# The second MLP matmul as seven half-size products (2x2 Strassen form) in a fused attention and MLP kernel

## The chip, the cores and the metric

The kernel runs on one core of a Trainium2 chip. The metric is the device time of one execution in microseconds (us), of which each kernel has several runs. A profile of one execution goes with it; its span (first to last instruction) is some 2 us shorter than the time (1.7 to 2.9 us in the runs of this study). Engines are named as the profile names them: PE is TensorE, PEld its weight loads, DVE is VectorE, ACT is ScalarE, POOL is GpSimd, SP is the engine that mostly issues DMAs.

## The reference

Eight batches of 576 rows go through an attention with separate softmaxes for q and k, then through a layer norm and a two-layer MLP with a residual. Cut to what matters:

```python
q_s = softmax(q, axis=-1)                 # q, k, v: (8, 8, 576, 64) fp32
k_s = softmax(k, axis=2)
x   = q_s @ (k_s^T @ v)                   # per batch and head, then (8, 576, 512)
xn  = (x - mean(x)) / sqrt(var(x) + 1e-6) * g_ln
out = x + maximum(xn @ w_ch1, 0.0) @ w_ch2   # w_ch1: 512 x 2048, w_ch2: 2048 x 512
```

## The kernel before

The rows are cut into nine chunks of 512. Chunks 0 to 7 hold the first 512 rows of each batch. Chunk 8 (`C9`) gathers the 64 rows that each batch has left over. For each chunk the first MLP matmul makes `ph = w1^T xn^T`, a ReLU writes it to `hT` (hidden index on the partitions, 16 slices of 128), and the second matmul takes slices of `hT` as weights against `w2_sb`. The attention work of the next chunk is issued in between as "side" work, at given places of the stream of matmuls.

```python
def cast_v(b, j, eng=None):               # fp32 v to bf16, for the k^T v product
    ...
    if eng is nc.scalar:
        nc.scalar.copy(dst, raws[b][1][:, hs])
    else:
        nc.vector.tensor_copy(out=dst, in_=raws[b][1][:, hs])

def stats(c, t, src):                     # layer norm of row tile t
    nc.vector.bn_stats(st[:, t], src)
    nc.vector.bn_aggr(mv[:, t], st[:, t])
    nc.vector.scalar_tensor_tensor(xn[:, t], in0=src, scalar=mv[:, t, 0:1], in1=g_bc, ...)

def y_out(c, t, pc, cols=slice(0, 512), eng=None):
    ...
    nc.vector.scalar_tensor_tensor(ot, in0=pc, scalar=rstds[c][:, t:t+1], in1=xs[c][0][:, t, cols], ...)
    eng = eng or nc.gpsimd
    if c < B:
        eng.dma_start(out[c, 0:SM, :].rearrange("(p t) n -> p t n", t=T)[:, t, cols], ot)
    else:                                  # chunk 8: 2 x 64 rows, one store for each batch
        for half in range(2):
            eng.dma_start(out[2*t + half, SM:S, cols], ot[64*half : 64*half + 64])

def mm2(c, t, ko):                         # 4 row tiles x 16 slices, 512 wide
    ...
    nc.tensor.matmul(hbox["pc"], hbox["h"][:, ko, t, :], w2_sb[:, ko, :],
                     start=(ko == 0), stop=(ko == KO2 - 1))
    if ko == KO2 - 1:
        y_out(c, t, hbox["pc"])

# main loop, chunk 1 (cut)
side += prep_side(2, 16, 46)               # exp of q and k, cast_v of batch 2
side += attn_side(2, 46, 62, 63, 87)       # attention of batch 2
side += [(40, lambda: load_batch(3))]
...
```

The last row tile of chunk 8 is done in two halves of 256 columns (`mm2_last`), so that little is left to store at the very end. POOL issues most stores.

The softmax here doesn't subtract the row's maximum and nothing guards it: scores larger than these inputs give would overflow.

## Time and profile before

| what | value | read from |
|---|---|---|
| time, median of 3 runs | 301.36 us (299.45 to 301.83) | times |
| span of the profiled run, granted clock | 297.7 us, 1.000 | page |
| PE busy | 284.4 us, 96% | page, part 1 |
| chunks 1 to 6 | 29.75 to 29.80 us each | start of each chunk's first matmul |
| chunk 7, chunk 8 | 29.38, 27.83 us | same |
| after the last matmul ("tail") | 4.24 us | same |

Parts 1 and 2 of the page of the kernel before. Each digit of a row of part 2 is a fortieth of the span, in tenths busy.

```profile
PE 284.4 (96%) x1679; PEld 147.3 (49%) x1697; DVE 179.7 (60%) x392; ACT 131.7 (44%) x242; POOL 30.8 (10%) x63
PE   6869988999999999999999999999999999999994
DVE  4556588437995975397539753975399258820021
PEclk9999999999999999999999999999999999999999
```

PE is the bound, at full clock, from chunk 1 (the eighth slice) on.

The next view cuts the same run into stretches, here chunk 1, chunk 3, chunk 8 and the tail. Its first line names the columns; a count of instructions stands in brackets.

```profile
core 0: us, PE busy (x) PEld busy (x) DVE busy (x) ACT busy (x) POOL busy (x), PEclk, DMA share, GB/s
57.53:87.28 29.75, 29.57 (x163) 14.48 (x164) 21.53 (x51) 17.49 (x34) 2.25 (x5) 1.00 0.79 221
...
117.08:146.87 29.79, 29.69 (x163) 14.47 (x164) 19.66 (x44) 13.64 (x25) 2.24 (x4) 1.00 0.92 221
...
265.63:293.46 27.83, 27.78 (x144) 13.98 (x143) 4.87 (x7) 8.36 (x14) 3.71 (x7) 1.00 0.16 38
293.46:297.70 4.24, 0.00 (x0) 0.00 (x0) 0.48 (x1) 0.00 (x0) 0.00 (x0) 0.98 0.28 63
```

PE has 0.1 to 0.2 us of idle time in a chunk of 29.8 us. DVE has 20 to 22 us of work in chunks 1 to 3.

Last, the tile query for `vm`, the bf16 copy of v, in chunks 1 and 2 (duration in ns as minimum, median, maximum):

```profile
L149 DVE CAST vm<-vt x12: 410/420/477, 64.0 to 108.4; 128x512 bf16<-128x512 f32 x12
```

### The profile page before, as it was taken

To read this page: it belongs to the slowest core of one execution; us is meant where nothing else is said; L and a number is where in the kernel's file an instruction comes from. 1 tells how busy PE (TensorE), PEld (TensorE's weight loads), DVE (VectorE), ACT (ScalarE), POOL (GpSimd) and SP (SyncE) were. 2 spreads that over 40 slices of the span, in tenths; PEclk is the share of its full clock that TensorE was granted. 3 is DMA by queue.
4 is the path that set the end of the run, shared out by engine and by line. 5 is a ranking of instruction groups with operands and counts; after the bars stand their busy time and mean duration, and the time that the engine had idled before them with its cause. 6 is when DMAs were issued, how large, how long until landed. Compare 5 with 4: busy or idle time off the path is not lost.

```text
span 297.7 us, 4354 instructions
## 1 busy us (share of the span) xinstructions
PE 284.4 (96%) x1679; PEld 147.3 (49%) x1697; DVE 179.7 (60%) x392; ACT 131.7 (44%) x242; POOL 30.8 (10%) x63
## 2 busy tenths in 40 slices
PE   6869988999999999999999999999999999999994
PEld 2658654445445444544454445444544444444443
DVE  4556588437995975397539753975399258820021
ACT  3538783396254560475047504750471054015300
POOL 3500020200010011001100110011000100110021
PEclk9999999999999999999999999999999999999999
DMA  7999999948968993999599629962017201120033
GB/s 195 216 208 271 289 157 237 318 139 242 296 138 222 333 138 128 306 262 184 130 309 223 124 90 311 221 141 73 35 35 124 90 35 37 53 88 35 2 70 70
DMA packets 73942, 48.97 MB, mean 164 GB/s; under 512 B 42241, under 2 KB 71681, under 8 KB 73922
## 3 DMA queue, kind: packets, MB, share of 16 engines
q1 hardware_dynamic: 66050, 34.74, 48.6%
q0 software_dynamic: 7872, 13.96, 18.9%
q8 instruction: 13, 0.21, 0.3%
q14 instruction: 7, 0.06, 0.1%
HBM read 36.70 MB, written 9.44 MB: 155 GB/s over the span
## 4 chain that ended last, share of the span: by engine, by line
PE 86%; DMA 5%; ACT 3%; DVE 3%; issue 1%; SPq 1%; POOL 0%; ACTq 0%
PE ph L344 37%; PE pc L393 36%; PE pc L404 3%; DMA qt<-in_q_dram 3%; PE pkv L241 2%; PE ph L359 2%; PE po L273 2%; DMA kt_98<-in_k_dram 2%; PE pc L415 1%; PE ptr L511 1%; DVE xn L299 1%; ACT ek L139 1%; DVE st L297 1%; PE po L280 1%; ACT hT L332 1%
## 5 line engine op out<-in xcount | busy, mean ns | idle before, releaser
L344 PE MATMUL ph<-xnT,w_sb 128*128 128x512 bf16 x528 | 128.1, 379 | 0.0
L332 ACT ACTIVATE hT<-ph 128x512 bf16<-128x512 f32 x115 | 68.4, 597 | 106.2 <-PE ph L344 106.1
L393 PE MATMUL pc<-w_sb,hT 128*128 128x512 bf16 x481 | 109.4, 379 | 0.7
L393 PEld LDWEIGHTS <-hT 128*128 128x128 bf16 x496 | 47.8, 98 | 58.3 <-DVE hT L330 2.3
L344 PEld LDWEIGHTS <-w_sb 128*128 128x128 bf16 x528 | 48.0, 98 | 50.5 <-DMA xnT<-xn 0.3
L375 DVE SCALAR_TENSOR_TENSOR ot<-pc,rstd,x 128x512 f32<-128x512 f32 (+1 forms) x37 | 27.1, 733 | 39.6 <-PE pc L393 31.2
L381 POOL DMA_DIRECT2D out_dram<-ot x32 | 18.1, 564 | 203.4 <-DVE ot L375 191.4
L273 PE MATMUL po<-kv_sb,eqT 128*128 128x128 bf16 x128 | 24.3, 219 | 1.5 <-DVE kv_sb L250 0.8
L189 DVE TENSOR_REDUCE zq<-eq 128x8 f32<-128x512 bf16 x34 | 22.4, 660 | 3.6 <-ACT eq L180 3.6
L330 DVE TENSOR_SCALAR hT<-ph 128x512 bf16<-128x512 f32 x17 | 11.7, 685 | 21.2 <-PE ph L344 21.1
L299 DVE SCALAR_TENSOR_TENSOR xn<-x,mv,g_bc 128x512 bf16<-128x512 bf16 x30 | 22.5, 752 | 1.1
L241 PE MATMUL pkv<-vm,ek 128*128 128x129 bf16 x112 | 22.6, 220 | 0.4 <-DVE vm L149 0.3
L297 DVE BATCH_NORM_STATS2 st<-x 128x6 f32<-128x512 bf16 x30 | 20.8, 694 | 1.0
L273 PEld LDWEIGHTS <-eqT 128*128 128x128 bf16 x128 | 11.7, 98 | 13.2 <-issue 1.9
L172 ACT ACTIVATE eq<-qt 128x512 bf16<-128x512 f32 x24 | 13.3, 619 | 10.4 <-DMA qt<-in_q_dram 10.4
L311 DVE TENSOR_TENSOR x<-po,rq 128x512 bf16<-128x512 f32 x26 | 17.8, 683 | 0.2
L404 PE MATMUL pc<-w_sb,hT 128*128 128x512 bf16 x61 | 15.6, 379 | 0.2
L139 ACT ACTIVATE ek<-kt 128x512 bf16<-128x512 f32 x28 | 15.5, 619 | 0.1
L247 DVE RECIPROCAL rzk<-pkv 128x2 f32<-128x2 f32 x14 | 2.4, 171 | 20.1 <-PE pkv L241 20.1
L149 DVE CAST vm<-vt 128x512 bf16<-128x512 f32 x26 | 10.2, 421 | 5.7 <-DMA vt<-in_v_dram 5.5
L468 PE MATMUL warm<-junk 128*128 128x256 bf16 (+1 forms) x59 | 11.0, 329 | 1.2 <-DVE junk L560 1.2
L241 PEld LDWEIGHTS <-ek 128*128 128x128 bf16 x112 | 10.6, 98 | 1.9 <-issue 0.8
(79 smaller groups left out, 178.3 us busy)
## 6 DMA issues: line engine op xcount, KB each, us to landing
out_dram<-ot POOLq DMA_DIRECT2D x32, 256.0 KB, 3.8
qt<-in_q_dram SPq DMA_DIRECT2D x7, 1024.0 KB, 12.5
vt<-in_v_dram SPq DMA_DIRECT2D x7, 1024.0 KB, 9.7
kt<-in_k_dram SPq DMA_DIRECT2D x6, 1024.0 KB, 7.5
w_sb<-in_moe_w_ch_dram POOLq DMA_DIRECT2D x8, 512.0 KB, 9.8
kt_98<-in_k_dram SPq DMA_DIRECT2D x4, 288.0 KB, 5.6
qt<-in_q_dram SPq DMA_DIRECT2D x2, 512.0 KB, 6.5
kt<-in_k_dram SPq DMA_DIRECT2D x2, 512.0 KB, 8.3
```

The lines of the kernel that those rows point to most:

```text
L139: nc.scalar.activation(eks[b][:, :, hs, :].rearrange("p t h d -> p h t d"), kt[:, hs], AF.Exp)
L189: nc.vector.reduce_sum(zq[:, t], eq[:, t], axis=AX.X)
L241: nc.tensor.matmul(pkv[:, j % 2, 0:w], lhsT, rhs, start=(t == 0), stop=(t == last))
L273: nc.tensor.matmul(pobox["p"][:, i * P : i * P + P], eqTs[c][:, t, i, :], kv_sb[:, c, i, :], start=True, stop=True,)
L297: nc.vector.bn_stats(st[:, t], src)
L299: nc.vector.scalar_tensor_tensor(xn[:, t], in0=src, scalar=mv[:, t, 0:1], in1=g_bc, op0=ALU.subtract, op1=ALU.mult,)
L332: nc.scalar.activation(dst, src, AF.Relu)
L344: nc.tensor.matmul(hbox["ph"], w1_sb[:, ko, m * P : (m + 1) * P], xnTs[c][:, :, ko, :], start=(ko == 0), stop=(ko == KO1 - 1),)
L375: nc.vector.scalar_tensor_tensor(ot, in0=pc, scalar=rstds[c][:, t : t + 1], in1=xs[c][0][:, t, cols], op0=ALU.mult, op1=ALU.add,)
L381: eng.dma_start(out[c, 0:SM, :].rearrange("(p t) n -> p t n", t=T)[:, t, cols], ot)
L393: nc.tensor.matmul(hbox["pc"], hbox["h"][:, ko, t, :], w2_sb[:, ko, :], start=(ko == 0), stop=(ko == KO2 - 1),)
L404: nc.tensor.matmul(hbox["pc", t], hbox["h"][:, ko, t, :], w2_sb[:, ko, :], start=(ko == 0), stop=(ko == KO2 - 1),)
```

## The change

For chunks 2 to 8 the second matmul is written as a 2x2 block product. Its blocks are the two halves of the rows, the even and odd slices of the contraction, and the two halves of the columns. The Strassen-Winograd form needs seven block products in place of eight. Each is 2 row tiles x 8 slices of matmuls 256 columns wide, so 64 matmuls of 512 columns become 112 of 256: seven eighths of the columns. The price is four sums of blocks of `hT` per chunk (on DVE, eight instructions), partial sums that ACT copies into other PSUM banks or SBUF and DVE adds, and, once for the whole kernel, four differences of blocks of `w2_sb` (on POOL, sixteen instructions). To find the memory, the buffers of k and v are single. The order of the side work is new, and so is the store of chunk 8. From chunk 2 on ACT also does the ReLUs that DVE had, and from batch 4 on the casts of v. The diff, cut to its core:

```diff
+    w2_q = const.tile([P, 4, KH, DH2], BF16)
...
+            raw.tile([P, H, T, D], FP32, tag="kt", name="kt", bufs=1),
+            raw.tile([P, H, T, D], FP32, tag="vt", name="vt", bufs=1),
...
+    def quarter_w2(i, g):                       # 16 times, in chunk 1
+        ...
+        dst, x, y = ((t1, b12, b11), (t3, b22, b12), (t2, b22, t1), (t4, b21, t2))[i]
+        nc.gpsimd.tensor_sub(out=dst, in0=x, in1=y)
...
+    def sum_h(g, i):                            # 8 times per chunk
+        dst, x, y, op = (
+            (s1, a21, a22, ALU.add), (s2, s1, a11, ALU.subtract),
+            (s3, a11, a21, ALU.subtract), (s4, a12, s2, ALU.subtract),
+        )[i]
+        nc.vector.tensor_tensor(out=dst, in0=x, in1=y, op=op)
...
+    def store_rest(eng, t, cols):               # chunk 8
+        eng.dma_start(out[2 * t : 2 * t + 2, SM:S, cols], ybox[C9, t][:, cols])
...
+        product(1, "a", first=True, at={
+            0: [lambda i=i: sum_h(1, i) for i in range(4)], 15: [seed_c]})
+        product(5, "b", first=True)
+        product(6, "a", at={15: [lambda: copy_u("s2")]})
+        product(2, "c", last=True, at={7: [seed_e]})
+        product(7, "a", at={2: ys("c", 0, 0)[:1], 5: ys("c", 0, 0)[1:], 15: [lambda: copy_u("s3")]})
+        product(3, "e", last=True, at={13: [lambda: add_u("b", "s3")]})
+        product(4, "a", last=True, at={
+            1: ys("e", 1, 0)[:1], 4: ys("e", 1, 0)[1:],
+            7: ys("b", 1, 2)[:1], 10: ys("b", 1, 2)[1:], 15: ys("a", 0, 2)})
...
             if c == 1:
                 side += prep_side(2, 16, 46)
                 side += attn_side(2, 46, 62, 63, 87)
+                side += [(40, lambda: load_batch(3, (2,))), (50, lambda: load_batch(3, (0, 1)))]
+                side += prep_side(3, 96, 127, sums=False)
+                side += [
+                    (4 + 7 * (4 * i + g), lambda i=i, g=g: quarter_w2(i, g))
+                    for i in range(4) for g in range(4)
+                ]
```

More of the change, by code (lines that the diff above doesn't have):

```diff
@@ L49 @@
     NP = H // 2
+    KH = KO2 // 2
+    DH2 = DM // 2
     VW = P + 2
     C9 = B
+    FAST = 2
     T0 = 6
@@ L73 @@
     ones_f = const.tile([1, P], FP32)
-    g_row = const.tile([1, DM], FP32)
-    v0 = const.tile([P, H, T0, D], BF16)
     g_bc = const.tile([P, DM], FP32)
@@ L101, in alloc_batch @@
         raws[b] = (
-            raw.tile([P, H, T, D], FP32, tag="kt", name="kt"),
-            raw.tile([P, H, T, D], FP32, tag="vt", name="vt"),
+            raw.tile([P, H, T, D], FP32, tag="kt", name="kt", bufs=1),
+            raw.tile([P, H, T, D], FP32, tag="vt", name="vt", bufs=1),
             raw.tile([P, H, T, D], FP32, tag="qt", name="qt"),
@@ L121, with load_qrem @@
     qrs = {}
-    def load_qrem(r):
-        qr = raw.tile([P, H, D], FP32, tag="qr", bufs=4, name="qr")
-        for half in range(2):
-            nc.sync.dma_start(
-                qr[SR * half : SR * half + SR],
-                q[2 * r + half, :, SM:S, :].transpose([1, 0, 2]),
-            )
-        qrs[r] = qr
+    def load_qrem():
+        qr = raw.tile([P, T, H, D], FP32, tag="kt", bufs=1, name="qr")
+        for r in range(T):
+            for half in range(2):
+                nc.sync.dma_start(
+                    qr[SR * half : SR * half + SR, r],
+                    q[2 * r + half, :, SM:S, :].transpose([1, 0, 2]),
+                )
+            qrs[r] = qr[:, r]
     eks, eqs, eqTs, xs, xnTs, rstds = {}, {}, {}, {}, {}, {}
@@ L207, in exp_k0 @@
         if j == 0:
-            eks[0] = raw.tile([P, T0, H, D], BF16, tag="vt", name="ek0")
+            eks[0] = raw.tile([P, T0, H, D], BF16, tag="vt", name="ek0", bufs=1)
         nc.scalar.activation(
@@ L214, in k0_mm @@
         hs = slice(2 * j, 2 * j + 2)
-        return eks[0][0:P0, t, hs, :], v0[0:P0, hs, t, :], P
+        return eks[0][0:P0, t, hs, :], raws["v0"][0:P0, hs, t, :], P
     def z0_mm(j):
@@ L326, in rstd_op, with relu @@
         nc.scalar.activation(rstds[c], lnv, AF.Exp, scale=-0.5)
-    def relu(i, dst, src):
-        if i % 8 == 7:
+    def relu(i, dst, src, fast):
+        if i % 8 == 7 and not fast:
             nc.vector.tensor_scalar_max(dst, in0=src, scalar1=0.0)
@@ L348, in mm1 @@
         if ko == KO1 - 1:
-            relu(m, hbox["h"][:, m], hbox["ph"])
+            relu(m, hbox["h"][:, m], hbox["ph"], c >= FAST)
     def mm1_part(c, m, t0, tn, ko):
@@ L409, in mm2_stream @@
             y_out(c, t, hbox["pc", t])
-    def mm2_last(c, t, half, ko):
-        if ko == 0:
-            hbox["pc"] = mm_ps.tile([P, DM], FP32, tag="m", name="pc")
-        cols = slice(256 * half, 256 * half + 256)
-        nc.tensor.matmul(
-            hbox["pc"][:, 0:256], hbox["h"][:, ko, t, :], w2_sb[:, ko, cols],
-            start=(ko == 0), stop=(ko == KO2 - 1),
-        )
-        if ko == KO2 - 1:
-            y_out(c, t, hbox["pc"][:, 0:256], cols, nc.sync)
+    def quarter_w2(i, g):
+        ks = slice(2 * g, 2 * g + 2)
+        rows = [w2_sb[:, 4 * g + odd : 4 * g + 4 : 2, :] for odd in range(2)]
+        (b11, b12), (b21, b22) = [(r[:, :, 0:DH2], r[:, :, DH2:DM]) for r in rows]
+        t1, t2, t3, t4 = [w2_q[:, n, ks, :] for n in range(4)]
+        dst, x, y = ((t1, b12, b11), (t3, b22, b12), (t2, b22, t1), (t4, b21, t2))[i]
+        nc.gpsimd.tensor_sub(out=dst, in0=x, in1=y)
@@ new lines, in h_part @@
+    def h_part(odd, half, ks=slice(0, KO2 // 2)):
+        rows = slice(2 * ks.start + odd, 2 * ks.stop, 2)
+        return hbox["h"][:, rows, 2 * half : 2 * half + 2, :].rearrange("p k t c -> p k (t c)")
+    def sum_h(g, i):
+        if g == 0 and i == 0:
+            hbox["s"] = mlp.tile([P, 4, KH, 2 * P], BF16, tag="hs", name="hs", bufs=1)
+        ks = slice(KH // 2 * g, KH // 2 * g + KH // 2)
+        s1, s2, s3, s4 = [hbox["s"][:, n, ks] for n in range(4)]
+        a11, a12, a21, a22 = [h_part(odd, half, ks) for half in range(2) for odd in range(2)]
+        dst, x, y, op = (
[3 more added lines that the diff above has]
+        nc.vector.tensor_tensor(out=dst, in0=x, in1=y, op=op)
@@ new lines, in prod @@
+    def prod(n, bank, t, k, first=False, last=False):
+        at = slice(t * P, t * P + P)
+        if n in (1, 2, 4):
+            odd, half = ((0, 0), (1, 0), None, (1, 1))[n - 1]
+            lhsT = hbox["h"][:, 2 * k + odd, 2 * half + t, :]
+        else:
+            lhsT = hbox["s"][:, {5: 0, 6: 1, 7: 2, 3: 3}[n], k, at]
+        if n in (1, 2):
+            rhs = w2_sb[:, 2 * k + n - 1, 0:DH2]
+        elif n == 3:
+            rhs = w2_sb[:, 2 * k + 1, DH2:DM]
+        else:
+            rhs = w2_q[:, {5: 0, 6: 1, 7: 2, 4: 3}[n], k]
+        nc.tensor.matmul(hbox[bank][:, t], lhsT, rhs, start=first and t == 0 and k == 0,
+                         stop=k == KH - 1, skip_group_check=True)
@@ new lines, in bank, with y_quarter @@
+    def bank(name):
+        hbox[name] = mm_ps.tile([P, 2, DH2], FP32, tag="m", name="b" + name)
+    def y_quarter(c, t, col, src):
+        if (c, t) not in ybox:
+            ybox[c, t] = outp.tile([P, DM], FP32, tag="ot", name="ot")
+            ynum[c, t] = 0
+        cols = slice(DH2 * col, DH2 * col + DH2)
+        nc.vector.scalar_tensor_tensor(
+            ybox[c, t][:, cols], in0=src, scalar=rstds[c][:, t : t + 1],
+            in1=xs[c][0][:, t, cols], op0=ALU.mult, op1=ALU.add,
+        )
+        ynum[c, t] += 1
+        if c == C9:
+            if t >= 2:
+                store_rest(nc.scalar if t == 2 and col == 0 else nc.sync, t, cols)
+            elif ynum[c, t] == 2:
+                store_rest(nc.sync, t, slice(0, DM))
+        elif ynum[c, t] == 2:
+            nc.gpsimd.dma_start(
+                out[c, 0:SM, :].rearrange("(p t) n -> p t n", t=T)[:, t], ybox[c, t]
+            )
@@ new lines, in store_rest, with copy_u, add_u, mm2_fast @@
+    def store_rest(eng, t, cols):
+        eng.dma_start(out[2 * t : 2 * t + 2, SM:S, cols], ybox[C9, t][:, cols])
+    ybox, ynum = {}, {}
+    def copy_u(name):
+        hbox[name] = mlp.tile([P, 2, DH2], FP32, tag=name, name=name, bufs=1)
+        nc.scalar.copy(hbox[name], hbox["a"])
+    def add_u(dst, src):
+        nc.vector.tensor_tensor(out=hbox[dst], in0=hbox["b"], in1=hbox[src], op=ALU.add)
+    def mm2_fast(c):
+        steps = []
+        def product(n, name, first=False, last=False, at=None):
+            at = at or {}
+            for t in range(2):
+                for k in range(KH):
+                    i = t * KH + k
+                    def go(t=t, k=k, i=i):
+                        if i == 0 and first:
+                            bank(name)
+                        prod(n, name, t, k, first, last)
+                        for fn in at.get(i, []):
+                            fn()
+                    steps.append((0.5, go))
+        def seed_c():
+            bank("c")
+            nc.scalar.copy(hbox["c"], hbox["a"])
+        def seed_e():
+            bank("e")
+            add_u("e", "s2")
+        def ys(name, col, t0):
+            return [lambda t=t: y_quarter(c, t0 + t, col, hbox[name][:, t]) for t in range(2)]
+        product(1, "a", first=True, at={
[8 more added lines that the diff above has]
+            7: ys("b", 1, 2)[:1], 10: ys("b", 1, 2)[1:], 15: ys("a", 0, 2)})
+        return steps
@@ L437, in mlp_steps @@
             ]
-        second = [(1, lambda t=t, ko=ko: mm2(c, t, ko)) for t in range(T) for ko in range(KO2)]
-        if c == C9:
-            second[-KO2:] = [
-                (0.5, lambda h=h, ko=ko: mm2_last(c, T - 1, h, ko))
-                for h in range(2) for ko in range(KO2)
-            ]
-        return first + second
+        if c >= FAST:
+            return first + mm2_fast(c)
+        return first + [(1, lambda t=t, ko=ko: mm2(c, t, ko)) for t in range(T) for ko in range(KO2)]
     def spread(fns, a, b):
@@ L468, in warm, with prep_side @@
             nc.tensor.matmul(w[:, 0:width], junk[:, 0:P], junk[:, 0:width], start=True, stop=True)
-    def prep_side(b, a0, a1):
+    def prep_side(b, a0, a1, sums=True):
         n = a1 - a0
@@ L476, in prep_side @@
         s += spread([lambda j=j: cast_v(b, j) for j in range(NP)], a0 + 0.1 * n, a0 + 0.5 * n)
-        s += spread([lambda t=t: sum_q(b, t) for t in range(T)], a0 + 0.5 * n, a1)
+        if sums:
+            s += spread([lambda t=t: sum_q(b, t) for t in range(T)], a0 + 0.5 * n, a1)
         return s
@@ L499, in attn_side, with prep_fast, sums_fast, attn_fast @@
         if not pe:
-            s.append((127, lambda: rstd_op(c)))
+            s.append((po1 + 20, lambda: rstd_op(c)))
+        return s
+    def prep_fast(b):
+        s = spread([lambda j=j: exp_q(b, j) for j in range(NP)], 40, 62)
+        s += [(63, lambda: eq_T(b)), (66, lambda: prep_kvrem(b))]
+        s += spread([lambda j=j: exp_k(b, j) for j in range(NP)], 70, 104)
+        s += spread([lambda j=j: cast_v(b, j, nc.scalar) for j in range(NP)], 75, 109)
+        return s
+    def sums_fast(c):
+        eq, zq, rq = eqs[c]
+        s = spread([lambda t=t: nc.vector.reduce_sum(zq[:, t], eq[:, t], axis=AX.X) for t in range(T)], 0, 12)
+        return s + [(12, lambda: nc.vector.reciprocal(rq, zq))]
+    def attn_fast(c):
+        s = sums_fast(c)
+        s += spread(
+            [lambda j=j, t=t: kv_mm(c, j, t) for j in range(NP) for t in range(T + 1)], 2, 20
+        )
+        s += [(21, lambda: start_x(c))]
+        for t, (p0, p1) in enumerate(((20, 26), (32, 40), (60, 70), (80, 92.5))):
+            s += spread([lambda t=t, i=i: po_mm(c, t, i) for i in range(NP)], p0, p1)
+            s += [(p1, lambda t=t: x_out(c, t))]
+        s += [(60, lambda: xn_T(c, 0, 2)), (101, lambda: xn_T(c, 2, 2)), (105, lambda: rstd_op(c))]
         return s
@@ L539, in first_batch @@
         k0, _, q0 = raws[0]
+        v0 = mlp.tile([P, H, T0, D], BF16, tag="hs", name="v0", bufs=1)
+        raws["v0"] = v0
+        g_row = outp.tile([1, DM], FP32, tag="ot", name="g_row")
         def load_q0(half):
@@ L633, in load_gated, with load_batch @@
                 load_kvrem(nc.sync, b)
-    def load_batch(b):
-        alloc_batch(b)
-        for tile_ in raws[b][:3]:
-            nc.vector.memset(tile_[0:1, 0, 0, 0:1], 0.0)
-        for which in range(3):
+    def load_batch(b, parts=(2, 0, 1)):
+        if b not in raws:
+            alloc_batch(b)
+        for which in parts:
+            nc.vector.memset(raws[b][which][0:1, 0, 0, 0:1], 0.0)
+        for which in parts:
             load_main(nc.sync, b, which, 0, H)
-        load_kvrem(nc.sync, b)
+        if 1 in parts:
+            load_kvrem(nc.sync, b)
     with tc.manual_schedule(
@@ L692 @@
                 side += attn_side(2, 46, 62, 63, 87)
-            elif c + 1 < B:
-                side += attn_side(c + 1, 2, 22, 26, 58)
-            else:
-                side += attn_side(C9, 0, 0, 12, 84)
-            if c + 2 < B:
-                side += [(40 if c == 1 else 1, lambda b=c + 2: load_batch(b))]
-                side += prep_side(c + 2, 96 if c == 1 else 66, 127)
-            if c == 3:
-                side += [(40, lambda: [load_qrem(r) for r in range(T)])]
+                side += [(40, lambda: load_batch(3, (2,))), (50, lambda: load_batch(3, (0, 1)))]
[4 more added lines that the diff above has]
+                ]
+            else:
+                if c + 1 < B:
+                    side += attn_fast(c + 1)
+                else:
+                    side += sums_fast(C9) + attn_side(C9, 0, 0, 14, 80)
+                side += [(33 + 3 * i, lambda i=i: sum_h(0, i)) for i in range(4)]
+                if c + 2 < B:
+                    side += [(1, lambda b=c + 2: load_batch(b))]
+                    side += prep_fast(c + 2)
             if c == B - 2:
+                side += [(1, load_qrem)]
                 side += spread([lambda r=r: exp_qrem(r) for r in range(T)], 66, 90)
-                side += spread([lambda r=r: sum_q(C9, r) for r in range(T)], 70, 100)
                 side += [(94, lambda: eq_T(C9))]
             run(mlp_steps(c), side)
-        run(mlp_steps(C9), [])
+        run(mlp_steps(C9), [(33 + 3 * i, lambda i=i: sum_h(0, i)) for i in range(4)])
 _INS = ['q', 'k', 'v', 'moe_g_ln', 'moe_w_ch1', 'moe_w_ch2']
```

## The prediction

> **What bounds the kernel now.** TensorE. The busy-time part of the page gives PE 96% of the 297.7 us span, the chain that ended last is 86% PE, and the clock row is full throughout. Cut by chunk (busy time per stretch), each of chunks 1 to 7 takes 29.4 to 29.8 us with PE busy for 29.3 to 29.7 us of it; DVE has 17.4 to 22.2 us there, ACT 8.9 to 17.5 us. So in chunks 2 to 8 every matmul column removed is time, until another engine becomes the limit.
>
> **What the change removes and adds on PE.** Per chunk, 64 products 512 wide become 112 that are 256 wide. In the chain of work, 64 back-to-back 512-wide matmuls take 13.81 us, 215.8 ns each. The 256-wide ones of the last row follow each other every 109.3 ns (timeline of the tail), each with its own 98 ns weight load, so weight loading does not bind. The second matmul goes from 13.81 to 112 x 109.3 ns = 12.24 us: 1.57 us saved per chunk, 11.0 us over seven.
>
> **What it adds elsewhere, per chunk.** DVE: eight 1024-element bf16 sums, two adds into PSUM (about 0.69 us each, like the other 512-wide fp32 PSUM ops), eight half-wide output ops (484 ns) for four of 747 ns. It loses two ReLUs (685 ns), four casts (421 ns) and three reciprocals. [...]DVE sums to about 25 us of a 28.2 us period: close to full, not the bound. ACT gains four casts, two ReLUs and three PSUM copies, about 20 us of 28.2.
>
> **How much is on the critical path.** The loop I worry about: last ReLU of a chunk (ACT late by about 1.4 us because exp_q shares it), four sums (2.8 us), normalisation of row 2 (2.3 us), a PSUM add (0.7 us), normalisation of row 3 (2.3 us): about 9.6 us after the first matmul ends; the transpose of xn lands 3.0 to 3.4 us after issue (DMA issues by tile), so 12.7 to 13.0 us, when the second matmul ends at 12.7 us. It just fits: 0 to 0.5 us of stall per chunk. Chunk 7, where DVE also has sixteen 420 ns scalings, may stall 1 to 2 us. At the end DVE has two more half rows queued: about 0.8 us. I subtract 2.5 us from 11.0, rounded.
>
> **Prediction.** 301.4 - 8.6 = 292.8 us, range 289.8 to 297.0. Faster by over 2%: 0.76; within 2%: 0.22; slower: 0.02.
>
> **What would show it.** Right: chunks 2 to 6 take 28.2 to 28.8 us each; the 256-wide group has 784 matmuls on the change's line and follows at 109 ns; the sums show about 0.69 us; DVE is 85 to 90% busy there; few PE waits on DVE or on the transpose of xn. Wrong: [...]the first matmul of each chunk waiting on xnT's DMA; PE waiting at the second product-sum for hs, or at po for kv_sb; chunks still at 29.5 us or more.
>
> **What would make it wrong.** [...]If qt lands late, exp_q holds up ACT and the ReLUs behind it. If all waits are hidden, 290 us.

## The result

The changed kernel takes 323.01 us (median of 4 runs, 322.75 to 323.24) against 301.22 us. The ratio is 1.073, with a 95% interval of 1.070 to 1.077. A ratio here is the mean time of one kernel's fast runs over that of the other's of the same rounds, so it is not quite the ratio of the medians quoted beside it. The change costs 7%, and the output is correct.

The profiled span went from 297.7 to 321.0 us. Cut at the first matmul of each chunk, it changed so:

| stretch | before, us | after, us | difference |
|---|---|---|---|
| start of chunk 1 | 57.53 | 59.09 | +1.6 |
| chunk 1 (not in block form) | 29.75 | 38.87 | +9.1 |
| chunk 2 | 29.80 | 30.04 | +0.2 |
| chunks 3 to 6, together | 119.17 | 113.42 | -5.8 |
| chunk 7 | 29.38 | 29.40 | 0.0 |
| chunk 8 | 27.83 | 26.20 | -1.6 |
| after the last matmul | 4.24 | 23.98 | +19.7 |

The start of chunk 1 moves by itself: it lay between 56.5 and 60.6 us in the profiles (E9's slow run left out). So there are two large losses to explain, both in stretches without a matmul of the block form, and the gain in chunks 3 to 6 is there. Chunks 2 and 7, which are in block form, show no gain; they stand 1.7 and 1.0 us above the 28.35 us of chunks 3 to 6.

Parts 1 and 2 of the page after:

```profile
PE 281.7 (88%) x2017; PEld 181.7 (57%) x2017; DVE 226.5 (71%) x441; ACT 158.7 (49%) x293; POOL 44.8 (14%) x73
PE   8879989968997999999999999999999989999000
DVE  5545786698999779779977977897787997234100
PEclk9979999996997999999999999999999999999655
```

PE has less to do (281.7 against 284.4 us, in spite of a lower clock in places) but its share fell to 88%. The PE row is empty in the last three slices and thin in the ninth, tenth and thirteenth.

The stretches of the run after that answer to those shown of before, chunk 1, chunk 3, chunk 8 and the tail, and chunk 2 with them.

```profile
core 0: us, PE busy (x) PEld busy (x) DVE busy (x) ACT busy (x) POOL busy (x), PEclk, DMA share, GB/s
59.09:97.96 38.87, 32.29 (x166) 15.35 (x164) 35.20 (x47) 17.83 (x34) 19.70 (x21) 0.91 0.56 155
97.96:128.00 30.04, 29.91 (x213) 19.84 (x213) 25.18 (x52) 17.90 (x34) 2.32 (x5) 0.94 0.77 186
128.00:156.35 28.35, 28.22 (x214) 19.18 (x213) 23.40 (x50) 18.06 (x34) 2.14 (x5) 1.00 0.78 196
...
270.82:297.02 26.20, 26.20 (x178) 17.11 (x175) 10.10 (x19) 11.29 (x19) 1.38 (x3) 1.00 0.11 41
297.02:321.00 23.98, 0.00 (x1) 0.00 (x0) 0.88 (x2) 0.00 (x0) 0.00 (x0) 0.56 0.13 44
```

In chunk 1, DVE shows 35.2 us of work for 47 instructions, where it had 21.5 us for 51. POOL shows 19.7 us. PE is idle for 6.6 us (38.87 - 32.29) and busy for 2.7 us more than before, at a mean clock of 0.91. In chunk 2 the whole lost gain is slower matmuls: PE is busy for 29.91 us at a mean clock of 0.94, where it needs 28.22 us at 1.00 in chunk 3. In the tail no engine works but DVE, for 0.88 us. A DMA share of 0.13 is worth two of the 16 DMA engines (0.13 x 16 = 2.1), at 44 GB/s.

What PE waited for in chunk 1 of the run after (total us, times, longest):

```profile
PE pkv L244 <- DVE vm L152: 4.3, 1, 4.3
PE ph L347 <- DMA xnT<-xn: 2.3, 1, 2.3
```

The timelines of POOL and of DVE in chunk 1 of the run after (start, duration of the row, engine, line, operation, count):

```profile
60.89 8.93 POOL L421 TENSOR_TENSOR w_q<-w_sb 128x512 bf16<-128x512 bf16 x8
69.79 3.36 POOL L421 TENSOR_TENSOR w_q<-w_sb,w_q 128x512 bf16<-128x512 bf16 x3
87.80 0.55 POOL L384 DMA_DIRECT2D out_dram<-ot  x1 [14.65 <-DVE ot L378]
88.36 3.37 POOL L421 TENSOR_TENSOR w_q<-w_sb,w_q 128x512 bf16<-128x512 bf16 x3
```

```profile
61.81 12.29 DVE L152 CAST vm<-vt 128x512 bf16<-128x512 f32 x3 [1.77 <-DMA vt<-in_v_dram]
...
89.08 3.22 DVE L302 SCALAR_TENSOR_TENSOR xn<-x,mv,g_bc 128x512 bf16<-128x512 bf16 x1
```

The first eleven differences run on POOL without a gap from 60.89 to 73.15 us. The first cast of v begins at 61.81. The tile query shows that one of these casts lasted 11.6 us:

```profile
L152 DVE CAST vm<-vt x8: 408/420/11623, 61.8 to 99.2; 128x512 bf16<-128x512 f32 x8
```

It was the first of the three, from 61.81 to 73.44 us, and ended 0.3 us after POOL's row. In the same way an `xn` operation that takes 0.75 us elsewhere lasts 3.22 us beside the three differences from 88.36 to 91.73. The held cast shows as a long instruction (11.62 us), not as a wait: it had its data, and the profile counts it as busy, within DVE's 35.2 us.

PE then loses in two ways. In the stretch from 72 to 80 us the granted clock is only 0.62, and in 98.6 to 102 us, at the start of chunk 2, after the wait for `xnT`, 0.51. More idle time (6.6 us against 0.2) and slower matmuls (2.7 us) make up the 9.1 us of chunk 1. It is no rule that a wait lowers the clock: in E12, below, PE waited 2.6 us at the same place, and chunk 2 ran at 1.00.

### The profile page after: what moved, and what is told of

Same layout as the page of the kernel before. It is cut to its first block, busy times and chain, and to the rows that moved or that the text cites. A ratio compares the mean times of both kernels' runs of the same rounds, so it can differ in the third digit from the quotient of the medians.

```text
span 321.0 us, 5125 instructions
## 1 busy us (share of the span) xinstructions
PE 281.7 (88%) x2017; PEld 181.7 (57%) x2017; DVE 226.5 (71%) x441; ACT 158.7 (49%) x293; POOL 44.8 (14%) x73
## 4 chain that ended last, share of the span: by engine, by line
PE 61%; DMA 15%; DVE 10%; SPq 3%; issue 2%; POOL 1%; DVEq 0%; POOLq 0%
PE ph L347 31%; PE ba L454 15%; DMA w_sb<-in_moe_w_ch_dram 6%; DMA kt<-in_k_dram 5%; PE be L454 4%; PE bc L454 4%; PE bb L454 4%; DVE vm L152 4%; DMA vt<-in_v_dram 4%; PE pkv L244 2%; DVE xn L302 2%; PE po L276 2%; SPq L113 2%; DVE st L300 1%; DMA xnT<-xn 1%
## 5 line engine op out<-in xcount | busy, mean ns | idle before, releaser
L335 ACT ACTIVATE hT<-ph 128x512 bf16<-128x512 f32 x129 | 76.7, 598 | 68.0 <-PE ph L347 67.9
L454 PEld LDWEIGHTS <-hs 128*128 128x128 bf16 x448 | 43.1, 98 | 5.7 <-DVE hs L438 0.8
L454 PEld LDWEIGHTS <-hT 128*128 128x128 bf16 x336 | 32.2, 98 | 4.3
L438 DVE TENSOR_TENSOR hs<-hT 128x1024 bf16<-128x1024 bf16 x28 | 19.2, 686 | 21.4 <-ACT hT L335 21.4
L454 PE MATMUL ba<-w_q,hs 128*128 128x256 bf16 x224 | 27.3, 273 | 0.0
L487 ACT COPY s<-ba 128x512 f32<-128x512 f32 x14 | 8.2, 585 | 24.9 <-PE ba L454 24.9
L152 DVE CAST vm<-vt 128x512 bf16<-128x512 f32 x10 | 17.4, 1781 | 1.8 <-DMA vt<-in_v_dram 1.8
L407 PE MATMUL pc<-w_sb,hT 128*128 128x512 bf16 x64 | 16.1, 379 | 0.1
L623 DVE TENSOR_REDUCE zq<-eq 128x8 f32<-128x512 bf16 x24 | 15.1, 692 | 0.0
L396 PE MATMUL pc<-w_sb,hT 128*128 128x512 bf16 x64 | 14.9, 379 | 0.0
L244 PEld LDWEIGHTS <-ek 128*128 128x128 bf16 (+1 forms) x136 | 12.8, 102 | 2.8 <-issue 0.8
```

The source lines that it names most:

```text
L244: nc.tensor.matmul(pkv[:, j % 2, 0:w], lhsT, rhs, start=(t == 0), stop=(t == last))
L335: nc.scalar.activation(dst, src, AF.Relu)
L407: nc.tensor.matmul(hbox["pc", t], hbox["h"][:, ko, t, :], w2_sb[:, ko, :], start=(ko == 0), stop=(ko == KO2 - 1),)
L438: nc.vector.tensor_tensor(out=dst, in0=x, in1=y, op=op)
L454: nc.tensor.matmul(hbox[bank][:, t], lhsT, rhs, start=first and t == 0 and k == 0, stop=k == KH - 1, skip_group_check=True)
```

## The experiments

Sixteen kernels were run. All gave correct output. Each has runs of the kernel before on the same chip beside it. Chunk lengths below come from each run's profile, read as in the table above.

### Theories

**A (tail).** The store of chunk 8 went from two transfers of 64 rows to one of 2 x 64 rows, and by this theory it is slow in this shape: the tail has a DMA share of 0.13 at 44 GB/s, against 0.28 at 63 GB/s in the kernel before. How many DMA engines carry such a store, no run shows. By the trace, 1.05 MB at the 49 GB/s that flow between 300 and 315 us take an estimated 21 us. The rival: the block form itself makes all outputs late, and any form of store would take long.

**B (chunk 1).** The differences on POOL hold up DVE: the cast of 0.42 us lasted 11.62 us, the `xn` of 0.75 us 3.22 us. In the simple form, such an instruction of DVE does not run while POOL works through a row of differences; below this is called the hold. By what mechanism, no run shows. The rivals: POOL's work delays POOL's own stores and what hangs on them; or the single buffers and later loads delay v, not POOL.

### E1 and E2: one suspect each

`e1_split_store` gives chunk 8 its two stores back. `e2_casts_on_act` moves the casts of `prep_side` to ACT and keeps the slow store.

```diff
# e1_split_store
-        eng.dma_start(out[2 * t : 2 * t + 2, SM:S, cols], ybox[C9, t][:, cols])
+        for half in range(2):
+            eng.dma_start(
+                out[2 * t + half, SM:S, cols], ybox[C9, t][64 * half : 64 * half + 64, cols]
+            )
# e2_casts_on_act
-        s += spread([lambda j=j: cast_v(b, j) for j in range(NP)], a0 + 0.1 * n, a0 + 0.5 * n)
+        s += spread([lambda j=j: cast_v(b, j, nc.scalar) for j in range(NP)], a0 + 0.1 * n, a0 + 0.5 * n)
```

> Only the stores of chunk 8 are changed back to two stores of 64 rows each, on the same queues as in the changed kernel. Theory S ([...]DMA share 0.13 and 50 GB/s in the 24 us after the last matmul): the end after the last matmul falls from 24 us to about 4 to 5 us, the time from 323 to about 303.5 us. Rival (the end is long because too many stores start late, or because the ACT queue is used for the first time): the end stays above 15 us, time above 314 us.

> The changed kernel with only the casts of v for batches 2 and 3 (chunk 1) moved from DVE to ACT; the block differences stay on POOL, all loads as they were. Theory P (a DVE cast that reads SBUF cannot run while POOL works through a row of two-input SBUF subtractions): chunk 1 falls from 40.9 to 30 to 32 us (one xn op may still be held up by about 2.5 us, off the critical path), the time from 323 to about 313 us. Rival L (chunk 1 is long because the single kt and vt buffers bring v of batch 2 late, at 61.8 us): the casts start no earlier on ACT, chunk 1 stays above 37 us, time above 319 us.

E1 took 305.02 us, ratio 1.014 (1.009 to 1.020). Its chunks are those of the change to 0.06 us; its tail is 7.8 us instead of 24.0, and not the 4 to 5 us that I expected:

```profile
294.48:302.30 7.82, 0.00 (x0) 0.00 (x0) 0.88 (x2) 0.00 (x0) 0.00 (x0) 0.69 0.58 134
```

The DMA share is now 0.58 and the rate 134 GB/s. So 16.2 us of the tail were there by one store's shape. (The medians differ by 18.0 us; the start of chunk 1 was 2.6 us earlier in this profile, by its usual scatter.)

E2 took 317.59 us. Chunk 1 fell from 38.9 to 34.1 us, which misses the 30 to 32 that I expected, as the time misses the 313. The casts no longer stood still, but the timeline of DVE shows what the edit had left in POOL's way (POOL's three differences ran there from 82.03 to 85.41):

```profile
82.74 3.23 DVE L302 SCALAR_TENSOR_TENSOR xn<-x,mv,g_bc 128x512 bf16<-128x512 bf16 x1
```

The `xn` operation was held as before, PE waited 2.3 us for its transpose and 1.7 us for ACT, which now had the casts as well. So moving the casts to ACT freed the casts alone.

### E3, E4 and E5: the suspects put into the kernel before

`e3_before_pool11` adds eleven differences of the same shape to chunk 1 of the kernel before, with results that nobody reads, all written to one scratch tile. `e5_before_pool11_ring` is the same with four scratch tiles in turn. `e4_before_rowpair` gives the kernel before the one store of 2 x 64 rows.

```diff
# e3_before_pool11, against the kernel before; for e5 the lines marked with 5 replace those marked with 3
+    scr = const.tile([P, 2, DM // 2], BF16)                       # 3
+    scr = const.tile([P, 4, 2, DM // 2], BF16)                    # 5
+    def pool_sub(i):
+        k = 4 * (i % 4)
+        nc.gpsimd.tensor_sub(
+            out=scr,                                              # 3
+            out=scr[:, i % 4],                                    # 5
+            in0=w2_sb[:, k : k + 4 : 2, 0 : DM // 2], in1=w2_sb[:, k + 1 : k + 4 : 2, 0 : DM // 2])
...
+            if c == 1:
+                side += [(4 + 7 * i, lambda i=i: pool_sub(i)) for i in range(11)]
# e4_before_rowpair, against the kernel before
-            for half in range(2):
-                eng.dma_start(
-                    out[2 * t + half, SM:S, cols], ot[64 * half : 64 * half + 64]
-                )
+            eng.dma_start(out[2 * t : 2 * t + 2, SM:S, cols], ot)
```

> The kernel before with only 11 POOL subtractions of the same shape (128x512, two inputs from the second weight in SBUF, result unused) added in chunk 1; everything else, two kt and vt buffers too, as before. Theory P: the first cast of batch 2 lasts about as long as the POOL row that is left when it starts, 9 to 12 us, chunk 1 grows by 8 to 11 us to about 39 us, time about 310 us. Rival L: casts keep 0.42 us, chunk 1 stays at 29.8 us, time 301 us.

> The kernel before with only the stores of chunk 8 changed from two of 64 rows to one of 2 x 64 rows (POOL queue for the first three row tiles, SP for the last). Theory S: the stores run at about 50 GB/s, so the 1 MB of chunk 8 needs some 21 us from about 283 us on; the end after the last matmul grows from 4.2 to 11 to 16 us and the time by 7 to 12 us, to about 308 to 313 us. Rival (not the form of the store): 301 us.

> As the run with 11 POOL subtractions in the kernel before, but they write four tiles in turn instead of one, so each waits for the one four back, which is long done, and not for the one just before it. There (waiting on each other) they took 1.26 us each and the DVE casts slipped in between, 1.37 us each, and no time was lost. Theory R (DVE gets no turn while POOL has its next instruction ready; a row without waits is one long hold): POOL ops 1.12 us each back to back, the first cast of batch 2 lasts 9 to 12 us, chunk 1 about 37 to 41 us, time about 308 to 314 us. Rival (the hold is for one instruction; the long cast in the changed kernel has another cause there): casts 1.4 us, time 301 us.

E4 took 306.21 us, ratio 1.018 (1.013 to 1.023). Its chunks are those of the kernel before, its tail is 11.0 us instead of 4.2. From the last matmul on, these are its stretches:

```profile
292.93:300.00 7.07, 0.00 (x0) 0.00 (x0) 0.48 (x1) 0.00 (x0) 0.00 (x0) 0.86 0.25 83
300.00:303.90 3.90, 0.00 (x0) 0.00 (x0) 0.00 (x0) 0.00 (x0) 0.00 (x0) 0.50 0.06 21
```

So the shape of the store costs time in either kernel, 5.0 us by the medians, where 7 to 12 were expected. It costs less because three of the four row tiles were ready, and stored, earlier; and the rate was higher than in the change, 83 GB/s at a DMA share of 0.25, worth four engines. Three of the five stores went through POOL's queue here, none in the change; no run shows whether that made the rate.

E3 contradicted the simple form of theory B: the time is unchanged, 301.11 us, ratio 1.000 (0.996 to 1.004), and chunk 1 takes 29.75 us. E5 took 307.82 us, ratio 1.025 (1.017 to 1.033), with 36.5 us in chunk 1. The two differ in one thing. With one scratch tile each difference has to wait until the one before it has written; with four it has not. First E3, then E5, POOL's and DVE's rows of the timeline:

```profile
60.42 13.81 POOL L87 TENSOR_TENSOR scr<-w_sb 128x512 bf16<-128x512 bf16 x11
...
61.04 3.43 DVE L156 CAST vm<-vt 128x512 bf16<-128x512 f32 x3 [1.48 <-DMA vt<-in_v_dram]
64.39 1.37 DVE L162 CAST vr<-vtr 64x512 bf16<-64x512 f32 x1
```

```profile
61.53 12.26 POOL L87 TENSOR_TENSOR scr<-w_sb 128x512 bf16<-128x512 bf16 x11
...
61.45 13.29 DVE L156 CAST vm<-vt 128x512 bf16<-128x512 f32 x3 [0.77 <-DMA vt<-in_v_dram]
```

In E3 a difference comes every 1.26 us (13.81 / 11), and DVE gets in between two of them: a cast takes 1.37 us, slow but bearable. In E5 one comes every 1.11 us, and DVE gets in nowhere until the row has ended. (By the record the long cast of E5 even began 0.08 us before POOL's first difference.) This pair is the strongest evidence. The same amount of work on POOL costs nothing or 6.7 us, by whether POOL must ever wait for itself. In this kernel it also rules out the rivals of B. In both runs the differences are over (74.2 and 73.8 us) before the next store is ready (80.6 and 88.5 us), so they delay no store; and both keep the double buffers and the old order of loads.

### E6, E7 and E8: three ways to take the hold away

All three keep the split store of E1. `e6_split_w2dve` puts the sixteen differences on DVE. `e7_split_paced` lets each difference wait for a ReLU, eight in chunk 1 and eight in chunk 2. `e8_split_chained` adds a copy of four elements behind each difference, which reads its result, so that POOL has to wait for itself.

```diff
# e6_split_w2dve (and the split store)
-        nc.gpsimd.tensor_sub(out=dst, in0=x, in1=y)
+        nc.vector.tensor_sub(out=dst, in0=x, in1=y)
# e7_split_paced (and the split store, and i = 2, 3 moved to chunk 2)
+        nc.gpsimd.tensor_copy(out=gate, in_=hbox["h"][:, 2 * (4 * i + g) % 16, 0, 0:4])
         nc.gpsimd.tensor_sub(out=dst, in0=x, in1=y)
# e8_split_chained (and the split store)
         nc.gpsimd.tensor_sub(out=dst, in0=x, in1=y)
+        nc.gpsimd.tensor_copy(out=gate, in_=dst[:, 0, 0:4])
```

> The changed kernel with stores of 64 rows and the 16 block differences of the second weight on DVE instead of POOL. Theory R: nothing holds the casts; the differences are about 0.42 us each[...], 6.7 us of DVE in chunk 1, which has room; chunk 1 29.8 to 31 us, first matmul of chunk 2 not late, span about 290 to 292 us, time about 293 to 295 us. Rival L (single kt and vt buffers bring v late): chunk 1 stays above 33 us, time above 297 us.

> The changed kernel with stores of 64 rows; block differences stay on POOL, but each is released by a ReLU (every second one of the first matmul; half of them in chunk 1, half in chunk 2). Theory R: a cast waits for one POOL op at most (1.2 us); chunk 1 29.8 to 31 us, chunk 2 28.4 to 29 us, time about 293 us.

> The changed kernel with stores of 64 rows; the 16 block differences stay on POOL where they were, and after each a 4-element POOL copy reads its result, so that POOL must wait for its own op before the next. Only that copy differs from the run that split the stores alone (305.0 us). Theory R: casts about 1.4 us each instead of one of 11.6 us, chunk 1 30 to 31 us, time about 293 to 295 us. Rival (one hold per instruction, and another cause for the long cast): no change, 305 us.

| kernel | median, us | ratio to before | chunk 1 | chunk 2 | tail |
|---|---|---|---|---|---|
| E1, for comparison | 305.02 | 1.014 | 38.9 | 30.1 | 7.8 |
| E6, on DVE | 298.46 | 0.994 (0.988 to 1.000) | 30.9 | 28.5 | 7.9 |
| E7, paced | 297.91 | 0.993 (0.986 to 0.999) | 29.7 | 31.0 | 7.9 |
| E8, chained | 297.88 | 0.993 (0.986 to 1.001) | 30.7 | 29.1 | 7.9 |

Three edits that have only the hold in common give back 6.6 to 7.1 us. E8 even adds work to POOL, and nothing but its copies sets it apart from E1. The times still miss the 293 to 295 us that I expected, by 2.9 us or more, and E7's chunk 2 misses the expected 28.4 to 29 us: PE waits there 1.9 us for the transpose of `eq` (`eqT`, the exponentials of q) and 0.3 us each for `xnT` and `hs`. E8's timeline:

```profile
59.22 1.17 POOL L421 TENSOR_TENSOR w_q<-w_sb 128x512 bf16<-128x512 bf16 x1
60.45 0.19 POOL L422 CAST gate<-w_q 128x4 f32<-128x4 bf16 x1
60.59 1.16 POOL L421 TENSOR_TENSOR w_q<-w_sb 128x512 bf16<-128x512 bf16 x1
...
61.58 2.08 DVE L152 CAST vm<-vt 128x512 bf16<-128x512 f32 x3 [3.21 <-DMA vt<-in_v_dram]
```

The three casts take 2.08 us in place of 12.29. In E6 a difference takes DVE 0.42 us against POOL's 1.15, so for this work POOL was the slower place as well.

What is left at this point: the tail is 3.6 us longer than before, chunk 7 gains nothing, and chunks 1 and 2 together take 59.4 to 60.7 us where 59.55 less one block gain, some 58.1 us, were to be hoped for.

### E9 to E12: the remainders, with three misses

`e9_queues` spreads chunk 8's stores over three issuing engines. `e10_early` also issues the differences earlier than chunk 1's stores and puts the casts of batch 3 on ACT. `e11_c9` also moves the statistics of chunk 8's row tile 2 behind the sums of chunk 7. `e12_pool_chunk0` is E8 with all differences issued in chunk 0, as soon as `w2_sb` has landed; they were meant to be out of chunk 1.

```diff
# e9_queues, against e8
-            if t >= 2:
-                store_rest(nc.scalar if t == 2 and col == 0 else nc.sync, t, cols)
-            elif ynum[c, t] == 2:
-                store_rest(nc.sync, t, slice(0, DM))
+            if t >= 2 and col == 1:
+                store_rest(nc.gpsimd, t, cols)
+            else:
+                store_rest(nc.scalar if (t, col) in ((1, 1), (2, 0)) else nc.sync, t, cols)
# e10_early, against e9
-                    (4 + 7 * (4 * i + g), lambda i=i, g=g: quarter_w2(i, g))
+                    (4 + 3.5 * (4 * i + g), lambda i=i, g=g: quarter_w2(i, g))
-                side += prep_side(3, 96, 127, sums=False)
+                side += prep_side(3, 96, 127, sums=False, eng=nc.scalar)     # casts on ACT
# e11_c9, against e10: x_out(C9, 2) no longer behind its last matmul, but at 66
+            s.append((66, lambda: x_out(c, 2)))
# e12_pool_chunk0, against e8: behind load_gated(2), in place of chunk 1
+        for i in range(4):
+            for g in range(4):
+                quarter_w2(i, g)
```

> The chained run (stores of 64 rows, POOL differences waiting on each other) plus one change: the stores of chunk 8 go out by half row tile as soon as they are ready and over three issuing queues (SP 8, ACT 4, POOL 4) instead of ten in a row on SP. In the chained run SP issued ten stores in 6.4 us, and the end came 7.8 us after the last matmul, against 4.2 us before the change. If the serial issue on SP is what is left of the tail, the tail falls to 4.5 to 5 us and the time by about 3 us, to 294.5 to 295.5 us. Rival (the stores themselves are slow, 1 MB at the end): tail stays at 7 us or more.

> As the run with three store queues, plus: all 16 block differences stand ahead of the stores of chunk 1 in the POOL queue (they run from about 60 to 80 us), and the casts of batch 3 (end of chunk 1) are on ACT. In the chained run chunks 1 and 2 together take 59.9 us where 58.2 was expected, with DVE's casts and sums late at the seam. Expected if that is the cause: 58.2 to 58.8 us for the two chunks, time lower by 1 to 1.5 us, about 293.5 us.

> As the one before, plus: in chunk 7 the statistics of row tile 2 are put behind the first sums of the second matmul instead of ahead of them on DVE. Chunk 7 takes 29.4 us in every version, where 28.3 was expected of it without stalls; DVE is the engine that the products wait for there. Expected: chunk 7 28.6 to 28.9 us, time lower by 0.5 to 0.8 us, about 292.8 us.

> The chained run with one change: the 16 block differences stand in POOL's queue right behind the loads of the second weight, so they run from about 46 us, in chunk 0, and are done at about 66 us. If the POOL work is what lengthens chunks 1 and 2, chunk 1 falls from 30.7 to 29.8 us and chunk 2 from 29.1 to 28.4 us, time about 1.5 us lower (span without the varying head). Rival (the single kt and vt buffers or the order of loads lengthen them): both stay within 0.3 us.

E9: the ratio is 0.988 (0.984 to 0.993), median 297.44 us. One of its six runs took 1022.6 us, and was the profiled one, so there is no use in its chunks. In that run the 512-wide matmuls show 1103 ns each where they show 379 to 386 in the others, from beginning to end, while the clock record says 1.00; chunks 3 to 6 take some 106 us each. It stays unexplained, and it is left out of the ratio, but not of the median. (So it is with all medians here: they are over all runs, the ratios over the fast ones.) E10 and E11 have the same stores and must answer for E9.

E10: 298.58 us, ratio 0.995. Its tail is 7.4 us and that of E11 6.9, so three queues gain 0.5 to 1.0 of the 3.6 us: a miss. The issue of stores is not what makes most of the tail. Chunk 1 takes 32.4 us and chunk 2 29.9: a miss too. With the casts on ACT, PE waits 1.6 us in chunk 2 for the transpose of `eq`.

E11: 298.02 us, ratio 0.992. Chunk 7 went from 29.40 to 28.86 us, as expected; the time, expected at about 292.8 us, did not follow. Here the order of DVE's work was the cause: the wait "PE bb on DVE hs" of 0.5 us, which the change shows in chunk 7, is gone.

E12: 297.50 us, ratio 0.990 (0.985 to 0.994). Chunk 2 is at 28.36 us, but chunk 1 at 32.5 us: a miss. The edit also did less than it was meant to. With a wait behind each, the differences ran from 46.47 to 68.70 us, so half of them still lay in chunk 1, which begins at 57.17, and three casts of v beside them took 0.95 to 1.38 us. E12 therefore does not show chunk 1 without the hold. PE's only wait there, of 2.6 us, is for the DMA that transposes `xn`, after POOL's row. The run without any difference on POOL is E6: its chunks 1 and 2 take 59.4 us, so some 1.3 us are lost there without the hold, but DVE has the differences to do.

### E13 to E16: chunk 8 as before, and where q is loaded

`e13_plain_last` is E8 with chunk 8's second matmul in the old form. `e14_best` joins E12, E13 and the edit that E11 adds to E10, and `e16_best_again` is E14 once more. `e15_early_q` is E14 with the load of q for batch 3 earlier in chunk 1.

```diff
# e13_plain_last, against e8
-        if c >= FAST:
+        if FAST <= c < C9:
             return first + mm2_fast(c)
...                                     # chunk 8: mm2 and mm2_last of the kernel before
# e15_early_q, against e14
-                side += [(40, lambda: load_batch(3, (2,))), (50, lambda: load_batch(3, (0, 1)))]
+                side += [(17, lambda: load_batch(3, (2,))), (50, lambda: load_batch(3, (0, 1)))]
```

> The chained run with one change: chunk 8 has the row-by-row second matmul of the kernel before, with its stores. If the block form itself makes the long end, by finishing every row tile in the last 4 us, then chunk 8 takes 27.8 us instead of 26.2 us and the end after the last matmul 4.2 to 4.4 us instead of 7.85 us: 2.0 us less in all. Rival (the end is long for some other reason in the changed kernel): the end stays above 6 us.

> Both of the above and the later statistics of row tile 2 in chunk 7. Sum of the terms against the kernel before: chunk 2 to 6 1.4 us each less, chunk 7 0.5 us less, chunks 1 and 8 and the end as before: 7.6 us less, about 293.5 us, ratio 0.975. If less comes of it, the terms do not add up and something moves between chunks.

> The joined kernel with one change: the load of q for batch 3 is issued at about 62 us instead of 69.5 us. If the loads of batch 3 in the way of the transpose of xn make chunk 2 late, chunk 1 falls from 32.4 to 29.8 to 30.3 us and chunk 2 from 30.0 to 28.4 to 28.8 us, and the time is about 293 to 294 us in all its fast runs. Rival (the seam has another cause): chunk 1 stays above 31.5 us, time 296 to 297 us.

> The joined kernel unchanged. If the seam depends on how the loads of batch 3 happen to land, chunks 1 and 2 together come out anywhere between 58.5 and 62.5 us, time 293 to 298 us as before; if it is fixed, they repeat 62.5 us within 0.3 us.

| kernel | median, us | ratio to before | chunk 1 | chunk 2 | chunk 7 | chunk 8 | tail |
|---|---|---|---|---|---|---|---|
| before | 300.74 (E13, E14), 300.92 (E15, E16) | 1 | 29.8 | 29.8 | 29.4 | 27.8 | 4.2 |
| E13 | 295.83 | 0.986 (0.982 to 0.991) | 32.7 | 29.2 | 29.4 | 27.8 | 4.3 |
| E14 | 296.84 | 0.983 (0.977 to 0.988) | 32.4 | 30.0 | 28.9 | 27.8 | 4.3 |
| E16 (= E14) | 296.27 | 0.986 (0.981 to 0.990) | 33.4 | 30.1 | 28.9 | 27.8 | 4.2 |
| E15 | 295.13 | 0.978 (0.971 to 0.985) | 30.4 | 30.1 | 28.9 | 27.8 | 4.2 |

E13 settles the tail. In block form chunk 8 takes 26.2 us plus a tail of 7.9 us; in the old form, with the old stores, 27.8 plus 4.3, which is about 2 us less, as expected. The timelines of DVE and SP at the end say why, first of the change, then of E13:

```profile
291.82 0.88 DVE L465 SCALAR_TENSOR_TENSOR ot<-bc,rstd,x 128x256 f32<-128x256 f32 x2 [0.43 <-PE bc L454]
...
295.31 0.88 DVE L465 SCALAR_TENSOR_TENSOR ot<-be,rstd,x 128x256 f32<-128x256 f32 x2 [0.43 <-PE be L454]
295.83 16.23 SPq L481 DMA_DIRECT2D out_dram<-ot  x5
296.11 0.87 DVE L465 SCALAR_TENSOR_TENSOR ot<-bb,rstd,x 128x256 f32<-128x256 f32 x2
297.06 0.88 DVE L465 SCALAR_TENSOR_TENSOR ot<-ba,rstd,x 128x256 f32<-128x256 f32 x2
```

```profile
286.64 0.75 DVE L378 SCALAR_TENSOR_TENSOR ot<-pc,rstd,x 128x512 f32<-128x512 f32 x1 [2.70 <-PE pc L396]
288.39 0.48 DVE L378 SCALAR_TENSOR_TENSOR ot<-pc,rstd,x 128x256 f32<-128x256 f32 x1 [1.00 <-PE pc L418]
288.90 2.85 SPq L389 DMA_DIRECT2D out_dram<-ot  x4
290.13 0.48 DVE L378 SCALAR_TENSOR_TENSOR ot<-pc,rstd,x 128x256 f32<-128x256 f32 x1 [1.26 <-PE pc L418]
```

The block form finishes no row tile before its sixth product has ended, 1.9 us before the last matmul. All of the chunk's 1 MB is stored within the end, where the row-by-row form has half a row tile left. (E13's time is less clear than its tail: its chunk 3, with the code of E8, took 29.3 us instead of 28.4.)

E14 fell short of the expected 293.5 us. In its profile, of a run marked slow, chunks 1 and 2 take 62.5 us, where by its terms they should take some 58.2; the other chunks and the tail are as expected. E16, the same kernel, took 63.5 us there. It does not repeat E14 within 0.3 us, and it lies above the 58.5 to 62.5 us that I expected if the landing of loads decides.

E15 is the fastest kernel, at 295.13 us. Whether the earlier q did it is not settled. Chunks 1 and 2 together take 60.5 us in its profile, against 62.5 in E14 and 63.5 in E16; but E8 and E13 run the same code there and take 59.9 and 61.8, and the intervals of E14, E15 and E16 overlap. E14 and E15 each have two runs marked slow, more than 1.5% above their own fastest, which the ratios leave out, and this flatters both; the profile of E14 fell in one of them, so E16 is the better one to compare. What the traces show is only which wait came last: in E14 PE waits 2.5 us for the transpose of `xn`; in E16, the same kernel, 3.5 us for an output operation of DVE, which stood behind casts that had waited 2.95 us for v to land; in E15 both are gone and a wait of 1.9 us for the transpose of `eq` stands in chunk 2. Chunk 2 of E14 and E16 has no wait of its own: PE is busy for 29.9 us of 30.0 at a mean clock of 0.94, as in the change, where 28.2 us at 1.00 are enough. The single buffers of k and v were not separated from the order of the loads, so the cause of the 2 to 3 us that the seam of chunks 1 and 2 keeps is open. No version beat the kernel before by a proven 2%.

## Why the prediction was wrong

Predicted were 292.8 us, in a range from 289.8 to 297.0; measured were 323.0 us. Point by point:

- **The bound and the saving on PE: right.** A product of sixteen 256-wide matmuls takes 1.75 us in the chain of work, 109 ns each. Chunks 3 to 6 take 28.35 to 28.36 us, inside the predicted 28.2 to 28.8. The saving is 1.44 us for each of them, against 1.57.
- **The sums on DVE: right.** They take 684 to 692 ns by the view of groups, against the 0.69 us of the prediction, on which its 2.8 us for four sums and its some 25 us of DVE rest; the trace of the kernel before had no such sum to show it. DVE is busy for 22.8 to 23.4 of 28.35 us, 81 to 83%, a little under the 85 to 90% predicted.
- **The loop over the sums and `xnT`: right.** PE does not wait in chunks 3 to 6, and it fits as narrowly as predicted: in chunk 3 the last transpose of `xn` is issued 3.2 us before the next chunk's first matmul, and in chunk 7, where the landing is recorded, a transpose took 3.0 us. Chunk 7 lost what it could have gained, as the warning about it said; E11 got back 0.5 us.
- **"What it adds elsewhere, per chunk": this step failed, because it stopped at what recurs.** The sixteen differences on POOL happen once, in chunk 1, and are not in the prediction at all. They cost 9 us there, more than the whole predicted gain. That POOL's unbroken row holds up DVE's casts is shown by E5 against E3 (chunk 1 of 36.5 against 29.75 us), and by E6, E7 and E8; by what mechanism, no run shows. The prediction does not mention POOL.
- **"At the end DVE has two more half rows queued: about 0.8 us": this step failed most; the tail grew by 19.7 us.** Of these, 16 us are the shape of the store (E1, and E4 for the sign), a line of the diff that I read as a tidier spelling. The other 3.6 us are there because the block form delivers all outputs at the end (E13). The DVE work that I did count, about 0.8 us, is in fact 0.88 us after the last matmul, where it was 0.48 before; what the sum left out is the store behind it.
- **"I subtract 2.5 us from 11.0": mis-sized.** Even with both faults mended, the terms are 1.44 us for each of chunks 2 to 6, 1.6 us for chunk 8, 0 for chunk 7, less 3.6 for the tail, which makes 5.2 us, not 8.5; and the seam of chunks 1 and 2 takes 2 us or so of that. E8, which is that kernel, measured 3.2 us by its medians (301.11 - 297.88).

## What to carry to other kernels

Cost what a change does once, and what it does to the last transfer, with the same care as what it does in every round, because a loop that got 5% faster was outweighed here by eleven instructions and one access pattern. Before giving "free" work to POOL, look for DVE instructions beside it like those held here, the cast of v (11.62 us for 0.42) and `xn` (3.22 us for 0.75), and if it must run there, make POOL wait between instructions, as in E8 (three casts in 2.08 us in place of 12.29), or do the work on DVE, as in E6 (0.42 us for a difference in place of 1.15). A form that saves arithmetic but finishes all its outputs together should not be used for the last piece of the program: here it cost about 2 us (E13).
